# PSUM banks for scores in a fused attention and gated FFN kernel: every score one slot behind an FFN chunk takes the FFN bank, and weight pieces lie three slots apart

## The chip, the cores and the metric

The kernel runs on one core of one Trainium2 chip. The number that counts is the device time of one launch in microseconds (us). The kernel before takes 1467.96 us (median of 3 runs, 1467.65 to 1468.54). All the rows come from one profiled execution of it, whose own time is 1467.12 us; its span from the first to the last instruction is 1465.3 us.

## The reference

All inputs are float32 in the reference, with batch 4, 3136 positions and model width 256:

```python
scores = (1 / S) * z @ z.T                  # z: (4, 3136, 64)
x = u * (max(scores, 0) ** 2 @ v)           # u, v: (4, 3136, 256)
h = max(x @ w_in, 0)                        # w_in: (256, 1024)
c = conv over positions of h, 3 taps, one filter for each of the 1024 channels
out = (h * sigmoid(c)) @ w_out              # w_out: (1024, 256)
```

## The kernel before, in words

**Tiling.** The queries of a batch are cut into 6 blocks of 512 and a rest of 64. For every block the kernel walks over the 25 key tiles of 128 positions. One key tile of one block is a *slot*, so the main loop has 4 x 6 x 25 = 600 slots, numbered k from 0. Slot 77 is the third slot of the fourth block (77 = 3 x 25 + 2). Products are made from a high and a low part in float32r, three matmuls for one (two for the scores, whose operands hold both parts).

**What one slot does.** The loop at the end of the kernel is a software pipeline written out by hand, and each engine keeps its order. In loop slot k, ScalarE (ACT) and VectorE (DVE) first split the squared score of tile k+2 into its high part `ah` (`split_hi`, L513) and its low part `al` (`split_lo`, a subtraction through the helper on L171). Then ReLU (`relu`, L489) and square (`square`, L504) are made of tile k+3. On TensorE (PE) come the output matmuls of an FFN chunk where one is due (`ffn_out`, L780 to L782), the six `av` matmuls of tile k (`attend`, L535), the two score matmuls of tile k+4 (`scores`, L409 and L410), and last the six input matmuls of an FFN chunk where one is due (`ffn_in`, L705 to L708). Many tiles below the diagonal are not computed: their scores come back turned from memory (DMA transposes), and then the slot has no score matmul.

**The FFN.** The FFN of a block runs in eight chunks of 128 channels during the slots of the next block. `FS = [2, 5, 8, 11, 15, 18, 21, 24]` says in which slot of the block a chunk's `ffn_in` stands. Its result stays in one PSUM bank: ReLU in the next slot, the three taps on it in the two slots after (ACT L744, DVE L749 twice), the sigmoid and the gate four slots behind `ffn_in` (ACT L756, DVE `ffn_gate` L763). The gate is the last that reads the bank.

**PSUM.** There are eight banks: two for `av`, two for the FFN output (`o0`, `o1`), two with the tag `s` and two with the tag `ph`. A score normally takes an `s` bank, which comes free when `split_lo` of its tile is done. FFN chunks take the `ph` banks in turn; so do, at a few places, three small users: `ring_score`, `early` and `rem_scores`. A matmul that opens a bank waits on PE for the last reader of the tile that held it before; behind it in PE's order everything waits.

**The weights.** They arrive as 64-bit floats. 16 pieces of 128 x 256 are converted during the first two blocks by `prep_w`, in five stages in successive slots: stage 0 is two integer operations on DVE (L316, L320), stage 1 two on ACT, stage 2 one or two on DVE (L328, L333), stages 3 and 4 are on GpSimd (POOL) and ACT. `WS` gives each piece's first slot. Its intermediate words lie in SBUF (`wr`) or, for the pieces before slot 22 and those in `W_B`, in a PSUM bank (`wp`). The pieces in `W_A` do the second half of stage 2 on ACT and POOL instead of DVE.

Of the kernel before, what the change touches and what calls it, by code (L numbers as in the profile page):

```python
# [8 lines left out]
F32 = mybir.dt.float32  # L9
# [3 lines left out]
U32 = mybir.dt.uint32  # L13
U64 = mybir.dt.uint64
AF = mybir.ActivationFunctionType
ALU = mybir.AluOpType
# [12 lines left out]
LA, LT, LS = 4, 3, 2  # L29
# [2 lines left out]


K_O = 35
Q0 = 3
C0 = [0, 1, 2, 3, 16, 17, 22, 23, 4, 5, 18, 19, 8, 9, 20, 21, 6, 7, 10, 11, 14, 15, 12, 13, 24]

# [12 lines left out]
WARM = 7  # L50
VO = 4
Z1 = -3
WS = [2, 6, 8, 12, 16, 19, 21, 25, 27, 33, 36, 38, 40, 41, 46, 52]
WST = [0, 1, 1, 2, 3]
W_E = ["GGGGGGGGGGGGGGGG", "AAAAAAAAAAAAAAAA"]
W_C = 7
W_A = [9, 14]
W_B = [6, 7]
SQ = [26, 46]
W_P = 22  # L60

# [18 lines left out]
def kernel(  # L80
# [10 lines left out]
    nc = tc.nc  # L91
# [29 lines left out]
    def own(b, q):  # L121
        return CB if b == 0 and q < Q0 else 0

# [180 lines left out]
    def prep_w(stage, what, i, e3=nc.gpsimd, e4=nc.scalar, bank=None, low=None):  # L304
        t, *me = wst[what, i]
        lo, hi = words(t)
        n = hi.shape[-1]
        if stage == 0:
            if not me:
                x = w_area(1, 3).rearrange("p (a d) -> p a d", a=2)  # L310
                me = [x[:, 0], x[:, 1]]
            m, e = me
            if bank is not None:
                m, e = bank[:, 0, :n], bank[:, 1, :n]
            wst[what, i] = [t, *me, m, e]
            nc.vector.tensor_scalar(  # L316
                out=e.bitcast(U32), in0=hi, scalar1=20, scalar2=0x7FF,
                op0=ALU.logical_shift_right, op1=ALU.bitwise_and,
            )
            nc.vector.tensor_single_scalar(out=m.bitcast(U32), in_=hi, scalar=0xFFFFF, op=ALU.bitwise_and)  # L320
            return
        m, e, pm, pe = me
        if stage == 1:
            m, e = pm, pe
            nc.scalar.activation(e.bitcast(I32), e.bitcast(I32), AF.Relu, scale=2.0**23, bias=ebias)
            nc.scalar.activation(m, m.bitcast(U32), AF.Copy, scale=2.0**-20, bias=1.0)
        elif stage == 2:
            nc.vector.scalar_tensor_tensor(  # L328
                out=e.bitcast(U32), in0=hi, scalar=0x80000000, in1=pe.bitcast(U32),
                op0=ALU.bitwise_and, op1=ALU.bitwise_or,  # L330
            )
            if low is None:
                nc.vector.scalar_tensor_tensor(out=m, in0=lo, scalar=2.0**-52, in1=pm, op0=ALU.mult, op1=ALU.add)  # L333
            else:
                nc.scalar.activation(lo.bitcast(F32), lo, AF.Copy, scale=2.0**-52)
                low.tensor_tensor(out=m, in0=lo.bitcast(F32), in1=pm, op=ALU.add)
        elif stage == 3:
            e3.tensor_tensor(out=m, in0=m, in1=e, op=ALU.mult)
        elif what == "in":
            m = m.rearrange("p (a n) -> p a n", a=DC)  # L340
            a, b = (w[:, :, i * P : (i + 1) * P] for w in (wih, wil))
            copy(e4, a, m)
            sub(nc.gpsimd, b, m, a)
        else:
            copy(e4, woh[:, i], m)
            sub(nc.gpsimd, wol[:, i], m, woh[:, i])
# [50 lines left out]
    def scores(k):  # L397
        blk, j, tr = at_slot(k)
        if tr or held(k) or side(k) == CB - 1:
            return  # L400

        if k < K_O and k % 2:
            tag, n = ("ph", 2) if k < NJ else (f"o{k // 2 % 2}", 1)
        else:
            tag, n = "s", 2
        s = ps.tile([P, 512], F32, tag=tag, name="s", bufs=n)
        w, c = slice(j * P, (j + 1) * P), own_cols(k)
        r = zq[blk][:, c] if blk == 1 else turned(zq[blk][:, c])
        nc.tensor.matmul(s[:, c], lhsT=zh[:, w], rhs=r, start=True, stop=False)  # L409
        nc.tensor.matmul(s[:, c], lhsT=zl[:, w], rhs=r, start=False, stop=True)  # L410
        sc[k] = s

    rl, pl, dq, dd, tp = {}, {}, {}, {}, {}


# [11 lines left out]
    def part(k):  # L427
# [3 lines left out]
        if x is not None and x < CB - 1:  # L431
            src = rl[k][:, (x + 1) * P : (x + 2) * P if x else NB]
        elif x is None and not (tr or r < (Q0 if b == q == 0 else q + 1) or (r == QB and q >= RB)):
            src = rl[k]
# [257 lines left out]
    ph, hb, cc, gg, po = {}, {}, {}, {}, {}  # L692
# [125 lines left out]
    ev = defaultdict(lambda: tuple([] for _ in range(6)))  # L818
# [7 lines left out]
    def at(slot, cls, fn, *args):  # L826
        ev[slot][cls].append((fn, args))
# [3 lines left out]
    for q in zs[2:]:  # L831
        s = min(C0.index(j) for j in range(q * CB, min(q * CB + CB, NJ))) - LA - 3
# [11 lines left out]
    for b in range(1, B):  # L844
        k0 = (b * QB - 1) * NJ
        for q in range(QB + 1):
            s = k0 - (QB - 2 - q) * NJ + (12 if q % 2 == 0 else 4)
            if q == QB - 2:
                s = k0 + 6
            elif q == QB - 1:  # L850
                s = k0 + NJ + 6
            elif q == QB:
                s = k0 + 9
            if b == 1 and q < 2:
                s = (Q0 - QB) * NJ + NJ + k0 + 4 + 8 * q
            at(s - 4, POST, load_z, b, q)
            at(s, POST, prep_z, q)
        last = {j: i for i, (j, _) in enumerate(ent[b - 1][QB - 1])}
        for j in range(0, NJ, 2):
            s = k0 + max(last[j] + 2, last.get(j + 1, 0) + 2, V0 + V1 * j // NJ)  # L860
            if j == NJ - 1:
                s = k0 + V0 - 2
# [5 lines left out]
    for blk in range(1, NBLK):  # L868
        s = blk * NJ + E3
# [4 lines left out]
    for blk in range(PK, NBLK):  # L874
        s = blk * NJ + (R_E if blk % QB == RB else E24[blk % QB])
# [5 lines left out]
    n = len(RN) - 1  # L881
    for b in range(B):
# [9 lines left out]
        for i in range(n + 1):  # L892
            s = k5 + (R_J + 2 * i + R_L * (i == n - 1) // 2 if i < n else R_D + 1) + 1
# [23 lines left out]
    for i, (_, what, f) in enumerate(sorted(need)):  # L917
        s = WS[i]
        at(s - 4, POST, load_w, what, f)
# [11 lines left out]
    for blk in range(NBLK - 1):  # L931
        k0 = (blk + 1) * NJ
        at(k0, C_GATE, gate_x, blk, G)
        at(k0 + XS, C_XS, split_x, blk, (V, G))
        for f in range(FC):
            s = k0 + FS[f]
            if s == NS - 1:
                break
            at(s, POST, ffn_halo, blk, f)
            at(s, PE1, ffn_in, blk, f)  # L940
            at(s + RELU, C_RELU, ffn_relu, blk, f)
            at(s + RELU, C_RELU, ffn_keep, blk, f)
            at(s + TAP, C_TAP, ffn_tap, blk, f)
            at(s + ST1, C_ST1, ffn_conv, blk, f, 1)
            at(s + ST2, C_ST2, ffn_conv, blk, f, 2)
            before_end(s + SIG, C_SIG, ffn_sig, blk, f)
            before_end(s + GATE, C_G, ffn_gate, blk, f, G)
            before_end(s + GHI, C_HI, ffn_hi, blk, f, A)
            before_end(s + GHI, PE1, ffn_lo, blk, f, G)
            before_end(s + OUT0, PE0, ffn_out, blk, f, 0)  # L950
            before_end(s + OUT1, PE0, ffn_out, blk, f, 1)
        if blk < NBLK - 2:
            at(s + EVAC, C_EV, evac, blk)
            at(s + EVAC + 2, POST, store, blk)
    at(NS - 2, POST, rem_x)

    def tail():
        blk, pre = NBLK - 1, NBLK - 2
# [97 lines left out]
    with tc.manual_schedule():  # L1056
# [8 lines left out]
        n = FC * KW  # L1065
# [6 lines left out]
        for k in range(-LA, NS):  # L1072
            e = ev[k]
            run(e[PRE])
            early = k + LT < K_O
            if early and 0 <= k + LT:
# [81 lines left out]
```

## Time and profile before

| what | value |
|---|---|
| median of 3 runs | 1467.96 us |
| the profiled execution: its own time / its span | 1467.12 / 1465.3 us |
| PE busy | 1451.6 us (99% of the span), 6781 matmuls |
| ACT, DVE, POOL busy | 1178.5, 1143.4, 864.0 us |
| granted TensorE clock | 1.000 of full speed |
| DMA | mean 140 GB/s |

Busy times overlap. A matmul is shown with its whole way through the array (0.38 us for 512 columns) while the next one already starts; so two starts that lie up to 0.38 us apart show no idle time, and short waits are read from the distance between starts.

### The profile page before, as it was taken

To read this page: it belongs to the slowest core of one execution; us is meant where nothing else is said; L and a number is where in the kernel's file an instruction comes from. 1 tells how busy PE (TensorE), PEld (TensorE's weight loads), DVE (VectorE), ACT (ScalarE), POOL (GpSimd) and SP (SyncE) were. 2 spreads that over 40 slices of the span, in tenths; PEclk is the share of its full clock that TensorE was granted. 3 is DMA by queue.
4 is the path that set the end of the run, shared out by engine and by line. 5 is a ranking of instruction groups with operands and counts; after the bars stand their busy time and mean duration, and the time that the engine had idled before them with its cause. 6 is when DMAs were issued, how large, how long until landed. Compare 5 with 4: busy or idle time off the path is not lost.

```text
span 1465.3 us, 22715 instructions
## 1 busy us (share of the span) xinstructions
PE 1451.6 (99%) x6781; PEld 1260.7 (86%) x6781; DVE 1143.4 (78%) x1776; ACT 1178.5 (80%) x2246; POOL 864.0 (59%) x1218
## 2 busy tenths in 40 slices
PE   9999999999999999999999999999999999999998
PEld 7778888888888888888888888888888888888887
DVE  8998777768787777767777877876778777787677
ACT  8878887878877877878888788787887777878767
POOL 7875656447866654545776654554586654554433
PEclk9999999999999999999999999999999999999999
DMA  6544666865445556678444555586644446567621
GB/s 198 164 132 104 153 142 156 169 150 138 147 134 142 135 132 157 138 149 178 133 149 132 138 140 134 140 172 138 157 149 137 132 122 150 129 132 168 133 63 37
DMA packets 432380, 205.24 MB, mean 140 GB/s; under 512 B 330753, under 2 KB 411905, under 8 KB 432257
## 3 DMA queue, kind: packets, MB, share of 16 engines
q1 hardware_dynamic: 431584, 203.40, 56.9%
q8 instruction: 53, 0.87, 0.3%
q14 instruction: 71, 0.57, 0.1%
q10 hardware_dynamic: 672, 0.40, 0.1%
HBM read 36.59 MB, written 86.90 MB: 84 GB/s over the span
## 4 chain that ended last, share of the span: by engine, by line
PE 87%; POOL 4%; ACT 3%; DVE 3%; issue 2%; DMA 0%; SPq 0%; ACTq 0%; POOLq 0%; DVEq 0%
PE av L535 46%; PE ph L708 5%; PE o L780 5%; PE o L782 5%; PE ph L705 5%; PE o L781 5%; PE ph L706 5%; PE s L409 4%; PE s L410 4%; PE av L617 1%; DVE ph L749 1%; POOL vv L171 1%; POOL pl L439 1%; ACT ph L744 1%; DVE al L171 1%
## 5 line engine op out<-in xcount | busy, mean ns | idle before, releaser
L535 PE MATMUL av<-ah,vv 128*128 128x512 f32 x2400 | 708.7, 379 | 1.4 <-ACT ah L513 0.7
L171 DVE TENSOR_TENSOR al<-s,ah 128x512 fp32r<-128x512 f32 x576 | 397.5, 690 | 225.4 <-PE av L535 116.8
L535 PEld LDWEIGHTS av<-ah,vv 128*128 128x128 f32 x2400 | 449.5, 189 | 64.9 <-ACT ah L513 1.1
L535 PE MATMUL av<-al,vv 128*128 128x512 f32 x1152 | 437.0, 379 | 0.4
L171 POOL TENSOR_TENSOR gl<-hb,gh 128x512 fp32r<-128x512 f32 x192 | 245.3, 1277 | 157.1 <-ACT gh L174 149.3
L749 DVE SCALAR_TENSOR_TENSOR ph<-hb,cw,ph 128x512 f32<-128x512 f32 x384 | 286.8, 747 | 9.4 <-ACT ph L744 9.0
L439 POOL COPY pl<-t 128x1024 uint16<-128x1024 uint16 (+1 forms) x257 | 260.9, 1017 | 2.2 <-DMA dq<-pl 1.1
L535 PEld LDWEIGHTS av<-al,vv 128*128 128x128 f32 x1152 | 217.7, 189 | 32.6 <-DVE al L171 1.8
L504 DVE TENSOR_TENSOR s<-s,t 128x512 f32<-128x512 f32 x275 | 191.8, 697 | 61.5 <-ACT t L489 60.8
L489 ACT ACTIVATE t<-s 128x512 f32<-128x512 f32 x277 | 166.1, 599 | 64.1 <-PE s L410 60.0
L513 ACT CAST ah<-s 128x512 fp32r<-128x512 f32 x277 | 163.3, 590 | 59.8 <-DVE s L504 59.5
L756 ACT ACTIVATE ph<-ph 128x512 f32<-128x512 f32 (+1 forms) x200 | 115.4, 577 | 78.1 <-DVE ph L749 74.7
L739 POOL COPY halo<-hb 128x2 f32<-128x2 f32 x160 | 31.1, 194 | 240.6 <-ACT hb L734 232.2
L484 ACT ACTIVATE s<-tp 128x512 f32<-128x512 f32 x278 | 165.3, 596 | 4.9 <-DMA tp<-dd 3.0
L705 PE MATMUL ph<-xh,wih 128*128 128x512 f32 x384 | 145.8, 380 | 1.1 <-DVE hb L763 1.1
L780 PE MATMUL o<-gh,wol 128*128 128x512 f32 x384 | 145.9, 380 | 0.0
L782 PE MATMUL o<-gl,woh 128*128 128x512 f32 x384 | 145.5, 379 | 0.0
L706 PE MATMUL ph<-xh,wil 128*128 128x512 f32 x384 | 145.5, 379 | 0.0
L781 PE MATMUL o<-gh,woh 128*128 128x512 f32 x384 | 145.5, 379 | 0.0
L744 ACT ACTIVATE ph<-hb,cw 128x512 f32<-128x512 f32 x192 | 133.7, 696 | 6.2 <-POOL halo L739 0.4
L763 DVE TENSOR_TENSOR hb<-ph,hb 128x512 f32<-128x512 f32 x192 | 131.8, 686 | 5.1 <-ACT ph L756 0.7
L734 ACT ACTIVATE hb<-ph 128x512 f32<-128x512 f32 x192 | 114.2, 595 | 17.7 <-PE ph L708 16.3
(138 smaller groups left out, 2091.3 us busy)
## 6 DMA issues: line engine op xcount, KB each, us to landing
dq<-pl SPq DMA_DIRECT2D x232, 256.0 KB, 2.7
st<-in_v_dram SPq DMA_DIRECT2D x48, 256.0 KB, 3.1
ut<-in_u_dram SPq DMA_DIRECT2D x24, 512.0 KB, 4.1
out_dram<-ob SPq DMA_DIRECT2D x19, 512.0 KB, 3.8
st<-in_z_dram SPq DMA_DIRECT2D x24, 256.0 KB, 3.2
sh<-sc SPq DMA_DIRECT2D x44, 128.0 KB, 2.4
dd<-pl SPq DMA_DIRECT2D x69, 64.0 KB, 2.2
dd<-pl SPq DMA_DIRECT2D x23, 192.0 KB, 2.4
```

The lines of the kernel that those rows point to most:

```text
L171: eng.tensor_tensor(out=out, in0=a, in1=b.bitcast(F32), op=ALU.subtract)
L439: nc.gpsimd.tensor_copy(pl[k], src.bitcast(U16).rearrange("p (n h) -> p h n", h=2))
L484: nc.scalar.activation(sc[k][:, :NB], tp[k], AF.Square, scale=SC1**-0.5)
L489: nc.scalar.activation(rl[k], sc[k][:, :NB], AF.Relu, scale=SC1)
L504: nc.vector.tensor_tensor(out=s, in0=s, in1=rl[k], op=ALU.mult)
L535: nc.tensor.matmul(o, lhsT=w[:, j, d], rhs=pairs(r), start=first and i == 0, stop=last and i == len(ops) - 1)
L705: nc.tensor.matmul(o, lhsT=wih[:, dc, w], rhs=pairs(xh[blk][:, dc]), start=(dc == 0), stop=False)
L706: nc.tensor.matmul(o, lhsT=wil[:, dc, w], rhs=pairs(xh[blk][:, dc]), start=False, stop=False)
L749: nc.vector.scalar_tensor_tensor(out=c, in0=hb[blk, f][:, k : e + k], scalar=cw[:, f, k : k + 1], in1=c, op0=ALU.mult, op1=ALU.add,)
L780: nc.tensor.matmul(o, lhsT=wol[:, f, d], rhs=pairs(h), start=(f == 0), stop=False)
L781: nc.tensor.matmul(o, lhsT=woh[:, f, d], rhs=pairs(h), start=False, stop=False)
L782: nc.tensor.matmul(o, lhsT=woh[:, f, d], rhs=pairs(l), start=False, stop=(f == FC - 1))
```

## The change

Scores: in the new function body of `scores`, a tile whose score stands in the slot directly behind an `ffn_in` (that slot is put into the set `gaps`) takes a `ph` bank instead of an `s` bank, in all blocks and for tiles above 35. A slot is taken out of the set again where one of the three small users of `ph` stands in it or beside it. In the built program 63 scores change their bank: most blocks with computed scores have some in their slots 0, 3, 9, 16 and 19. What each of them waits for changes with it: one in a `ph` bank waits for the gate (`ffn_gate`) of the FFN chunk that held that bank; the next `ffn_in` into that bank, two slots on, waits for `split_lo` of the score; and the scores that stay in `s` banks meet a turn that is one slot longer. No matmul, vector or scalar operation is added or removed, and PE's order stays as it was.

Weights: pieces 8, 9, 10, 12, 13 and 14 (counted from 0) start in other slots: 27, 33, 36, 40, 41, 46 become 28, 31, 35, 41, 44, 47. Pieces 8 and 9 keep their intermediate words in a `ph` bank too. For the pieces in `W_A` the mantissa is written to SBUF in stage 1.

```diff
+GAPS = 99
-WS = [2, 6, 8, 12, 16, 19, 21, 25, 27, 33, 36, 38, 40, 41, 46, 52]
+WS = [2, 6, 8, 12, 16, 19, 21, 25, 28, 31, 35, 38, 41, 44, 47, 52]
-W_B = [6, 7]
+W_B = [6, 7, 8, 9]
...
         if stage == 1:
-            nc.scalar.activation(m, m.bitcast(U32), AF.Copy, scale=2.0**-20, bias=1.0)
+            nc.scalar.activation(me[0] if low else m, m.bitcast(U32), AF.Copy, scale=2.0**-20, bias=1.0)
...
-                low.tensor_tensor(out=m, in0=lo.bitcast(F32), in1=pm, op=ALU.add)
+                low.tensor_tensor(out=m, in0=lo.bitcast(F32), in1=m, op=ALU.add)
...
-        if k < K_O and k % 2:
+        if k - LA in gaps and k > K_O:
+            tag, n = "ph", 2
+        elif k < K_O and k % 2:
             tag, n = ("ph", 2) if k < NJ else (f"o{k // 2 % 2}", 1)
         else:
             tag, n = "s", 2
...
+    gaps = set()
...
             at(s, PE1, ffn_in, blk, f)
+            if blk < GAPS:
+                gaps.add(s + 1)
...
+    for s in list(gaps):
+        if any(fn in (ring_score, early, rem_scores) for x in (s - 1, s, s + 1) for c in ev[x] for fn, _ in c):
+            gaps.discard(s)
```

On DVE, from slot 41 to the start of slot 43, the order before holds the second half of piece 12 and the whole of piece 13 (`al` is the split that frees a score's bank; `wr` are words of a weight piece):

```order
L171 TENSOR_TENSOR al<-s,ah 128x512
L504 TENSOR_TENSOR s<-s,t 128x512
L328 SCALAR_TENSOR_TENSOR wr<-wr 128x256
L333 SCALAR_TENSOR_TENSOR wr<-wr 128x256
L316 TENSOR_SCALAR wr<-wr 128x256
L320 TENSOR_SCALAR wr<-wr 128x256
L171 TENSOR_TENSOR al<-s,ah 128x512
L504 TENSOR_TENSOR s<-s,t 128x512
L749 SCALAR_TENSOR_TENSOR ph<-hb,cw,ph 128x512
L328 SCALAR_TENSOR_TENSOR wr<-wr 128x256
L333 SCALAR_TENSOR_TENSOR wr<-wr 128x256
L171 TENSOR_TENSOR al<-s,ah 128x512
```

In the order now, the same stretch holds piece 12 alone (the changed file's lines are up to 4 higher):

```order
L172 TENSOR_TENSOR al<-s,ah 128x512
L508 TENSOR_TENSOR s<-s,t 128x512
L317 TENSOR_SCALAR wr<-wr 128x256
L321 TENSOR_SCALAR wr<-wr 128x256
L172 TENSOR_TENSOR al<-s,ah 128x512
L508 TENSOR_TENSOR s<-s,t 128x512
L753 SCALAR_TENSOR_TENSOR ph<-hb,cw,ph 128x512
L329 SCALAR_TENSOR_TENSOR wr<-wr 128x256
L334 SCALAR_TENSOR_TENSOR wr<-wr 128x256
L172 TENSOR_TENSOR al<-s,ah 128x512
```

What stands directly ahead of the last split is the same in both: a tap and two operations of a weight piece.

On DVE from slot 31 to 34, before, piece 9 begins near the end of the stretch (`hb<-ph,hb` is the gate of an FFN chunk, `ph<-hb,cw,ph` a tap):

```order
L763 TENSOR_TENSOR hb<-ph,hb 128x512
L171 TENSOR_TENSOR al<-s,ah 128x512
L504 TENSOR_TENSOR s<-s,t 128x512
L749 SCALAR_TENSOR_TENSOR ph<-hb,cw,ph 128x512
L171 TENSOR_TENSOR al<-s,ah 128x512
L504 TENSOR_TENSOR s<-s,t 128x512
L749 SCALAR_TENSOR_TENSOR ph<-hb,cw,ph 128x512
L316 TENSOR_SCALAR wr<-wr 128x256
L320 TENSOR_SCALAR wr<-wr 128x256
L171 TENSOR_TENSOR al<-s,ah 128x512
L504 TENSOR_TENSOR s<-s,t 128x512
L763 TENSOR_TENSOR hb<-ph,hb 128x512
```

Now piece 9 stands two slots earlier there, with its words in a PSUM bank (`wp`):

```order
L767 TENSOR_TENSOR hb<-ph,hb 128x512
L317 TENSOR_SCALAR wp<-wr 128x256
L321 TENSOR_SCALAR wp<-wr 128x256
L172 TENSOR_TENSOR al<-s,ah 128x512
L508 TENSOR_TENSOR s<-s,t 128x512
L753 SCALAR_TENSOR_TENSOR ph<-hb,cw,ph 128x512
L329 SCALAR_TENSOR_TENSOR wr<-wr,wp 128x256
L172 TENSOR_TENSOR al<-s,ah 128x512
L508 TENSOR_TENSOR s<-s,t 128x512
L753 SCALAR_TENSOR_TENSOR ph<-hb,cw,ph 128x512
L172 TENSOR_TENSOR al<-s,ah 128x512
L508 TENSOR_TENSOR s<-s,t 128x512
```

The two operations of stage 0 moved ahead of two splits, and that of stage 2 follows them; behind slot 52 DVE's order is unchanged.

## Rows read from the trace of the kernel before

**Rows 1.** The page's busy times of the engines, share of the span, instructions:

```profile
PE 1451.6 (99%) x6781; PEld 1260.7 (86%) x6781; DVE 1143.4 (78%) x1776; ACT 1178.5 (80%) x2246; POOL 864.0 (59%) x1218
```

**Rows 2.** Waits of PE: total us, times, longest us:

```profile
PE s L409 <- DVE al L171: 2.7, 4, 1.6
```

**Rows 3.** Windows: stretch, length, busy us of each engine (instructions), clock, DMA:

```profile
62.00:98.00 36.00, 33.71 (x151) 27.28 (x149) 34.65 (x61) 29.78 (x62) 24.49 (x37) 1.00 0.46 130
98.00:122.00 24.00, 23.54 (x109) 19.86 (x108) 21.22 (x33) 20.00 (x41) 20.23 (x28) 1.00 0.45 132
```

**Rows 4.** Timeline, a short wait in slot 152: start us, us, instruction:

```profile
358.64 0.69 DVE L171 TENSOR_TENSOR al<-s,ah 128x512 fp32r<-128x512 f32 x1
...
359.39 0.48 PE L409 MATMUL s<-zq,zh 128*128 128x512 f32 x1
...
359.71 0.38 PE L410 MATMUL s<-zq,zl 128*128 128x512 f32 x1
```

**Rows 5.** Timeline, a longer wait in slot 190:

```profile
453.36 0.69 DVE L171 TENSOR_TENSOR al<-s,ah 128x512 fp32r<-128x512 f32 x1
...
453.57 0.38 PE L535 MATMUL av<-al,vv 128*128 128x512 f32 x1
...
454.10 0.48 PE L409 MATMUL s<-zq,zh 128*128 128x512 f32 x1
...
454.42 0.38 PE L410 MATMUL s<-zq,zl 128*128 128x512 f32 x1
```

**Rows 6.** Timeline, slots 75 to 77:

```profile
180.41 0.68 DVE L763 TENSOR_TENSOR hb<-ph,hb 128x512 f32<-128x512 f32 x1
...
181.59 0.38 PE L409 MATMUL s<-zq,zh 128*128 128x512 f32 x1
...
184.94 0.69 DVE L171 TENSOR_TENSOR al<-s,ah 128x512 fp32r<-128x512 f32 x1
...
185.26 0.38 PE L705 MATMUL ph<-xh,wih 128*128 128x512 f32 x1
```

**Rows 7.** Timeline, slot 377:

```profile
898.47 0.69 DVE L171 TENSOR_TENSOR al<-s,ah 128x512 fp32r<-128x512 f32 x1
898.58 0.38 PE L705 MATMUL ph<-xh,wih 128*128 128x512 f32 x1
```

**Rows 8.** Timeline, slot 218:

```profile
520.29 0.69 DVE L171 TENSOR_TENSOR al<-s,ah 128x512 fp32r<-128x512 f32 x1
...
520.92 0.38 PE L705 MATMUL ph<-xh,wih 128*128 128x512 f32 x1
```

**Rows 9.** Timeline, slot 150:

```profile
354.60 0.68 DVE L763 TENSOR_TENSOR hb<-ph,hb 128x512 f32<-128x512 f32 x1
...
355.29 0.38 PE L409 MATMUL s<-zq,zh 128*128 128x512 f32 x1
```

**Rows 10.** Line 316: duration ns min/median/max, first and last start us, forms:

```profile
L316 DVE TENSOR_SCALAR wp<-wr x8: 418/469/506, 15.0 to 57.0; 128x256 uint32<-128x256 uint32 x8
L316 DVE TENSOR_SCALAR wr<-wr x8: 307/476/1310, 61.7 to 126.1; 128x256 uint32<-128x256 uint32 x8
```

**Rows 11.** Timeline, the largest wait, slots 38 and 39:

```profile
88.15 1.31 DVE L316 TENSOR_SCALAR wr<-wr 128x256 uint32<-128x256 uint32 x1
...
90.85 0.51 PE L409 MATMUL s<-zq,zh 128*128 128x512 f32 x1 [1.65 <-DVE al L171]
```

**Rows 12.** Timeline, slots 42 and 43:

```profile
99.89 0.87 POOL L236 CAST zq<-zh 64x512 fp32r<-64x512 f32 x1
...
100.06 1.06 DVE L328 SCALAR_TENSOR_TENSOR wr<-wr 128x256 uint32<-128x256 uint32 x1
...
101.06 1.08 DVE L333 SCALAR_TENSOR_TENSOR wr<-wr 128x256 f32<-128x256 uint32 x1
...
101.49 0.38 PE L705 MATMUL ph<-xh,wih 128*128 128x512 f32 x1
...
102.06 0.67 DVE L171 TENSOR_TENSOR al<-s,ah 128x512 fp32r<-128x512 f32 x1
```

## The prediction

> **What bounds the kernel now.** I read the page's busy times first. PE is busy 99% of the span, the other engines 59 to 80% [rows 1]. So nothing makes this kernel faster but taking away moments in which PE stands, and every new wait of PE is paid in full. Next the list of PE's waits: the one that counts is a score waiting for `split_lo` on DVE, that is for an `s` bank, 2.7 us in four long waits [rows 2]. That list is not the whole bill, since starts are 0.216 us apart where nothing waits (23.54 busy us for 109 matmuls [rows 3]) while one matmul is shown for 0.38 us; a start that comes 0.1 us late shows no idle time. I therefore went on to the timeline and took the distances from start to start.
>
> Two short pieces of it give the price of a late bank. In slot 152 the split ends at 358.64 + 0.69 = 359.33 and the score starts at 359.39: 0.06 us from release to start. It did not come late, yet the next matmul follows 0.32 us behind instead of 0.22, so 0.10 us is lost [rows 4]. In slot 190 the split ends at 454.05; the score starts 0.53 us after the `av` matmul ahead of it, 0.31 late, and again 0.10 is lost behind it [rows 5]. So a bank that comes free x us after the moment at which PE would have opened it costs x + 0.06 + 0.10 us; with x between -0.16 and -0.06 it costs the part of the 0.10 that is not hidden; below that nothing.
>
> Where PE loses time today: between 62 and 98 us, block 1 with weight pieces 8 to 13, 151 matmuls x 0.216 = 32.6 of 36 us; between 98 and 122, 109 x 0.216 = 23.5 of 24 [rows 3]. Some of these matmuls are half as wide, and start to start, slot by slot, the two stretches lose 4.0 and 1.0 us. All later blocks together lose only some 2.5 us at such places, outside the tail. DVE is busy for 34.65 of the first 36 us [rows 3]: there it is the bound.
>
> **The change part by part: scores and chunks in steady state.** No work is added or removed; 63 scores get another releaser, and so do the `ffn_in` two slots behind them. I took from the built program which tile held each bank before, and set the end of its last reader, as the trace has it, against the start on PE. Behind slot 53 all engines keep their order, so the same trace serves for both.
>
> The moved scores themselves mostly have room. In slot 75 the gate ends at 181.09 and the score starts at 181.59, 0.50 us of room [rows 6]. The `s` scores gain a turn: their room grows from 0.1 to 2 us now to 2.5 to 4. What is late next is `ffn_in`, whose bank was free for 4 us before and now waits for the split of the score that stood there two slots earlier. Slot 2 of a block is where DVE and ACT also prepare the next FFN input. In slot 77 the split ends at 185.63 and `ffn_in` starts at 185.26 [rows 6]: 0.37 + 0.16 = 0.53 us. Slots 227 and 527 have the same figures; in 377 it is 899.16 against 898.58, 0.58 + 0.16 = 0.74 [rows 7]. Sum of the four: 2.3 us. In slot 218 the split ends at 520.98 against 520.92: 0.06 + 0.16 = 0.22, and slots 368 and 518 repeat it: 0.7 [rows 8]. In slot 150 a moved score starts at 355.29 and its gate ends at 355.28: 0.15 us, five times (150, 300, 325, 450, 475): 0.75 [rows 9]. Slots 177, 327 and 477 stand as slot 152 does today, 0.10 each, and four more scores (153, 175, 303, 453) lose about 0.04: 0.45 together. Sum: 4.2 us. Against it go today's short waits that the longer turn removes: 152, 302, 452 (0.10 each), 55 (0.26), 205 and 355 (0.15 together): 0.7. The wait in slot 190 and its like in 340 stay: the tile before them in the bank is still two scores back. Net +3.5 us. What would hide a part: a shift of the DVE chain against PE by 0.4 us; I know of none, since DVE's order there is the same and its splits themselves follow PE's `av` matmuls. Bounds: +2.5 (the fifteen small ones cost nothing) to +4.5.
>
> **Block 1.** By the split of slot 40 the pieces 8 to 11 are done, before and now, so a DVE that is busy 96% of the time has the same work to do by then, and the 4.0 us lost there can shrink only by its idle 1.35 us [rows 3] and by operations that take less time. The latter is real but uncertain: an operation on `wr` takes between 0.31 and 1.31 us, median 0.48, one with its result in a PSUM bank always 0.42 to 0.51 [rows 10]. The largest wait, 1.65 us of idle in slot 39, follows one of 1.31 us [rows 11], 0.8 over the median. Pieces 8 and 9 in `ph` banks are safe from that, 10 and 11 meet other neighbours: I take -1.1 (0 to -2.4). Piece 9 stands two slots earlier, 0.8 us ahead of two splits for which slots 32 and 33 still wait in `s` banks; this is paid early and given back by slot 40. The moved scores of slots 34 and 37 want a gate that stands late in its slot on DVE, and the score's own split then starts later: +0.6. Sum to slot 40: -0.5, from -3.0 to +1.5.
>
> Slot 43 is new. Its `ffn_in` starts at 101.49 today; now it waits for the split that ends at 102.06 + 0.67 = 102.73, 1.24 + 0.16 = 1.4 us [rows 12]. That split is late because two operations of a weight piece ahead of it take 1.06 and 1.08 us beside casts of POOL [rows 12]; by the order lists two of the same kind still stand there, of piece 12 now instead of 13. With the median of some 0.48 each the wait would be 0.2. I take 1.2, nearer the row. The Trainium skill (SBUF — State Buffer, section Who interferes with whom) says that a DVE instruction with two SBUF inputs and a GpSimd instruction that reads SBUF share a port pair, and that the one that issues second is fully blocked. The trace agrees with the 1.06 and 1.08 us beside POOL's casts [rows 12]. By that rule the full 1.4 us come back, since POOL's casts are still issued there, and the sum would be 0.2 us higher; without it, 1 us lower.
>
> In slots 44 to 49 the 1.0 us lost today came with pieces 12 and 13 close together; with 13 three slots later most of it goes, and I keep 0.4: -0.6. Slots 50, 52 and 53 get 0.2. The changed stage 1 of the `W_A` pieces writes the same 256 columns to SBUF instead of PSUM: nothing, within 0.1 us on ACT, which is 80% busy; hidden by PE unless DVE waits for it. The moved loads of weight pieces on SP's queue lie four slots ahead of their use as before. Sum for block 1: -0.5 + 1.2 - 0.6 + 0.2 = +0.3, from -4 to +3.5.
>
> **The sum.** +3.5 + 0.3 = +3.8 us on the profiled execution's 1467.12 gives 1470.9. That execution lies 0.84 us below the median of the runs shown (1467.96), and the runs after will be compared with those: 1471.8 us.
>
> **The rivals.** *Block 1 pays for it.* The spread of the pieces takes all 5.0 us of stalls away and slot 43 meets no late split, while the steady cost stands: -5.0 + 3.5 = -1.5, 1466.5 us, no change. For it: block 1 holds two thirds of what PE loses today. Against: DVE's 34.65 of 36 us. *The third bank does its work.* It is the other side: the split of slot 77 and its like end 0.5 us earlier against PE, because ACT writes the turned tiles into `s` banks that now come free sooner, and block 1 runs clear: -5.0 - 0.7 = -5.7, 1462.3 us. It is decided at one point, whether the split of slot 77 still ends after 185.2. Against it: ahead of that split ACT runs without a pause, so a bank that is free sooner does not start it sooner. The Trainium skill (Perfetto Trace Analysis, section Optimization Strategy) says that consistent bubbles on the engine that should be saturated can mean too little PSUM for the next tile. That speaks for this rival; here such bubbles in steady state are 2.5 us, and by the rule 0.7 to 2.5 of them would go. *Block 1 gets worse.* In slots 34 to 46 score and chunk wait for each other's DVE work in the same `ph` banks, each wait delays the ReLU and square that follow, and DVE stands idle where it was saturated: +3.0 over the forecast, 1474.8 us. For it: piece 9 is earlier in the most loaded stretch. That the banks are not used as said is no rival: the built program shows the 63 places.
>
> **How the numbers follow.** The forecast (the sum, 1470.3 to 1473.6) gets 0.60, no net change 0.19, the third bank 0.08, the worse block 1 0.13. 0.2% is 2.9 us, about what a measurement of this kernel can tell from no change: slower means above 1470.9, faster below 1465.0. A fifth of the forecast's chance lies under 1470.9. So slower 0.48 + 0.13 = 0.61, same 0.12 + 0.19 = 0.31, faster 0.08. The range takes in the case of no net change and most of the worse block: 1466.0 to 1474.6, with 0.08 left below and 0.1 above.
>
> **What the profile after would show.** Right: waits of `ph` L709 (`ffn_in`) for DVE `al` in slots 77, 227, 377 and 527 of 0.4 to 0.6 us, and one near 1.2 us in slot 43; the waits of `s` scores in slots 35, 36, 39, 46, 55 and 152 gone; from 122 us to the tail the stretch longer by 3 to 4 us at the same matmul count. Wrong: no wait at slot 77, or block 1 shorter or longer by over 2 us.

## The result, and the profile after

The changed kernel takes 1476.19 us (median of 5 runs, 1475.18 to 1476.48), the kernel before 1467.65 us on the same chip (5 runs, 1467.40 to 1468.54). The ratio is 1.0053, with a 95% interval of 1.0041 to 1.0066: slower by 8.5 us. Forecast were 1471.8 us and a range that ended at 1474.6; the direction came out, the size lies outside. The profiled execution took 1476.48 us, its span is 1474.7 us.

The page's busy times answer to [rows 1]:

```profile
PE 1455.7 (99%) x6781; PEld 1259.3 (85%) x6781; DVE 1145.7 (78%) x1776; ACT 1179.4 (80%) x2246; POOL 864.2 (59%) x1218
```

The instructions are the same in number on every engine. DVE's work grew by 2.3 us. The list of PE's waits answers to [rows 2] (total us, times, longest us):

```profile
PE ph L709 <- DVE al L172: 3.8, 7, 1.2
PE s L412 <- DVE al L172: 3.5, 6, 1.5
...
PE s L412 <- DVE hb L767: 0.4, 1, 0.4
```

`ffn_in` (L709) now waits for splits, seven times; before, the list had no such line. But the scores (L412) wait longer for splits as well, 3.5 instead of 2.7 us. The windows answer to [rows 3]:

```profile
62.00:98.00 36.00, 31.62 (x139) 25.57 (x140) 31.98 (x54) 27.79 (x58) 22.32 (x35) 1.00 0.37 107
98.00:122.00 24.00, 22.11 (x99) 17.85 (x98) 21.87 (x34) 18.13 (x38) 16.79 (x23) 1.00 0.44 132
```

In the same 36 us PE issues 139 matmuls instead of 151, and DVE, which was busy for 34.65, is busy for 31.98: it has more idle time, not less.

From here on, "lost" is the distance from one matmul's start to the next beyond 0.216 us for 512 columns, summed by slot; a long wait comes out some 0.3 us above the idle time that the profile prints. In the two profiled executions slots 26 to 53 (block 1) lose 6.2 us before and 10.6 after, the later slots up to the tail 5.4 and 10.3. The spans differ by 9.4 us where the medians differ by 8.5; some single slots (446, 274, 574) lose anything between 0 and 0.8 us from one profiled execution to the next, also where the kernels do not differ, and the profile of before happened to have nothing at 446.

**The steady places.** Three timelines of after answer to [rows 6, 8, 9] (slots 77, 218, 150):

```profile
189.34 0.69 DVE L172 TENSOR_TENSOR al<-s,ah 128x512 fp32r<-128x512 f32 x1
...
190.09 0.48 PE L709 MATMUL ph<-xh,wih 128*128 128x512 f32 x1 [0.27 <-DVE al L172]
...
190.41 0.38 PE L710 MATMUL ph<-xh,wil 128*128 128x512 f32 x1
```

```profile
525.48 0.69 DVE L172 TENSOR_TENSOR al<-s,ah 128x512 fp32r<-128x512 f32 x1
...
526.23 0.48 PE L709 MATMUL ph<-xh,wih 128*128 128x512 f32 x1
...
526.55 0.38 PE L710 MATMUL ph<-xh,wil 128*128 128x512 f32 x1
```

```profile
359.52 0.68 DVE L767 TENSOR_TENSOR hb<-ph,hb 128x512 f32<-128x512 f32 x1
...
360.26 0.48 PE L412 MATMUL s<-zq,zh 128*128 128x512 f32 x1
```

Each starts 0.06 us behind the end of its releaser (190.03, 526.17, 360.20), and the next matmul stands 0.32 us behind instead of 0.22 (in slot 150 at 360.58): the price rule of the prediction. Lost are 0.53, 0.23 and 0.15 us.

**Block 1.** PE's waits there, from the timeline:

```profile
73.63 0.50 PE L412 MATMUL s<-zq,zh 128*128 128x512 f32 x1 [1.47 <-DVE al L172]
...
79.68 0.50 PE L412 MATMUL s<-zq,zh 128*128 128x512 f32 x1 [0.38 <-DVE hb L767]
...
84.88 0.48 PE L709 MATMUL ph<-xh,wih 128*128 128x512 f32 x1 [1.17 <-DVE al L172]
...
95.92 0.50 PE L412 MATMUL s<-zq,zh 128*128 128x512 f32 x1 [0.96 <-DVE al L172]
...
105.11 0.48 PE L709 MATMUL ph<-xh,wih 128*128 128x512 f32 x1 [1.06 <-DVE al L172]
...
121.59 0.48 PE L412 MATMUL s<-zq,zh 128*128 128x512 f32 x1 [0.41 <-DVE al L172]
```

These are slots 32, 34, 36, 40, 43 and 49; shorter ones of 0.33 and 0.32 us stand in slots 33 and 46. The wait of 1.65 us in slot 39 [rows 11] is gone; these took its place. What DVE does ahead of two of them, and where it stands idle in between:

```profile
64.85 0.70 DVE L508 TENSOR_TENSOR s<-s,t 128x512 f32<-128x512 f32 x1 [0.80 <-ACT t L493]
...
68.12 0.69 DVE L172 TENSOR_TENSOR al<-s,ah 128x512 fp32r<-128x512 f32 x1 [0.64 <-ACT ah L517]
...
71.38 0.68 DVE L767 TENSOR_TENSOR hb<-ph,hb 128x512 f32<-128x512 f32 x1
72.10 0.43 DVE L317 TENSOR_SCALAR wp<-wr 128x256 uint32<-128x256 uint32 x1
72.56 0.43 DVE L321 TENSOR_SCALAR wp<-wr 128x256 uint32<-128x256 uint32 x1
72.89 0.68 DVE L172 TENSOR_TENSOR al<-s,ah 128x512 fp32r<-128x512 f32 x1
...
81.14 0.70 DVE L508 TENSOR_TENSOR s<-s,t 128x512 f32<-128x512 f32 x1 [0.76 <-ACT t L493]
81.75 0.75 DVE L753 SCALAR_TENSOR_TENSOR ph<-hb,cw,ph 128x512 f32<-128x512 f32 x1
82.40 0.77 DVE L317 TENSOR_SCALAR wr<-wr 128x256 uint32<-128x256 uint32 x1
83.09 1.14 DVE L321 TENSOR_SCALAR wr<-wr 128x256 uint32<-128x256 uint32 x1
84.15 0.68 DVE L172 TENSOR_TENSOR al<-s,ah 128x512 fp32r<-128x512 f32 x1
```

The split at 72.89 follows a gate and the first two operations of piece 9, which now stand in this slot; it ends at 73.57 and PE starts at 73.63. The split at 84.15 has 1.9 us of piece 10 directly ahead of it.

The idle times of DVE have two causes. That at 64.85 comes before any new wait of PE: piece 8 starts a slot later now, DVE and ACT have less to do there, get ahead, and ACT waits for a score that PE makes in its turn. Before, DVE stood 0 us there, and 0.49 at the place of 68.12. The run piece8_only, which moves piece 8 alone, has both idle times. First ACT's row in the changed kernel, then DVE's in piece8_only:

```profile
64.22 0.60 ACT L493 ACTIVATE t<-s 128x512 f32<-128x512 f32 x1 [0.70 <-PE s L413]
```

```profile
65.11 0.70 DVE L508 TENSOR_TENSOR s<-s,t 128x512 f32<-128x512 f32 x1 [0.70 <-ACT t L493]
...
68.33 0.69 DVE L172 TENSOR_TENSOR al<-s,ah 128x512 fp32r<-128x512 f32 x1 [0.59 <-ACT ah L517]
```

The idle time at 81.14 comes behind PE's wait in slot 34: there the score itself is late, then ACT's `t`, then DVE.

### The profile page after: what moved, and what is told of

It reads as the page before. It is cut to its first block, busy times and chain, and to the rows that moved or that the text cites. A ratio compares the mean times of both kernels' runs of the same rounds, so it can differ in the third digit from the quotient of the medians.

```text
span 1474.7 us, 22671 instructions
## 1 busy us (share of the span) xinstructions
PE 1455.7 (99%) x6781; PEld 1259.3 (85%) x6781; DVE 1145.7 (78%) x1776; ACT 1179.4 (80%) x2246; POOL 864.2 (59%) x1218
## 4 chain that ended last, share of the span: by engine, by line
PE 84%; ACT 6%; DVE 4%; issue 2%; POOL 2%; DMA 1%; SPq 0%; ACTq 0%; POOLq 0%; DVEq 0%
PE av L539 44%; PE ph L709 5%; PE ph L712 5%; PE o L786 5%; PE o L784 5%; PE o L785 5%; PE ph L710 5%; PE s L412 4%; PE s L413 4%; PE av L621 2%; DVE al L172 1%; DVE ph L753 1%; ACT t L493 1%; ACT xh L175 1%; ACT ah L517 1%
## 5 line engine op out<-in xcount | busy, mean ns | idle before, releaser
L709 PE MATMUL ph<-xh,wih 128*128 128x512 f32 x384 | 147.4, 384 | 5.0 <-DVE al L172 3.8
L738 ACT ACTIVATE hb<-ph 128x512 f32<-128x512 f32 x192 | 114.3, 596 | 17.1 <-PE ph L712 15.8
```

Source lines behind the costliest of these rows:

```text
L709: nc.tensor.matmul(o, lhsT=wih[:, dc, w], rhs=pairs(xh[blk][:, dc]), start=(dc == 0), stop=False)
```

## The experiments

All are the changed kernel with other constants, and some with one line changed as shown; "old" and "new" are the two lists `WS` of the diff above, and `W_B` is that of before unless it is said. The changed stage 1 of the `W_A` pieces is in all of them. Each was compared with the kernel before on the same chip. The lost times are those of one profiled execution of each kernel.

**Which half, and which blocks.** Four kernels:

```diff
weights_only:      WS new, W_B = [6, 7, 8, 9], GAPS = 0
banks_only:        WS old, GAPS = 99
block1_only:       WS new, W_B = [6, 7, 8, 9], GAPS = 1   # moved scores in block 1 alone
banks_later_only:  WS old
-            if blk < GAPS:
+            if 1 <= blk < GAPS:
```

> The new weight slots and the new W_B, every score in its old bank (GAPS = 0). Theory A, the weight slots cost in block 1 by themselves: piece 9 two slots earlier meets the stretch in which DVE is already the bound, and pieces 8 and 9 keep a ph bank from ffn_in. Then slots 30 to 33 lose 2 us more than before, as in the changed kernel, nothing changes behind slot 55, and the time is +2 to +4 us on before. Theory B, the banks cost in block 1: slots 30 to 33 recover in the slots behind them, and the time is within 1 us of before. Theory C, only both together cost: slots 30 to 33 lose 2 us and slots 36 to 49 win as much: within 1 us too, but with the loss of slots 30 to 33 in the trace.

> The moved scores in all blocks, the weight pieces in their old slots and banks. The steady cost that was read off the trace before (+3.5 us net behind slot 53) comes back to within 0.5 us, slot 77 losing 0.53. Theory A: block 1 stays where it was or better, so +3 to +4 us in all. Theory B: block 1 loses 3 to 4 us as in the changed kernel, +7 to +8 in all. Theory C: in between, and slot 43 loses over 1 us.

> The new weight slots, scores moved only behind the FFN chunks of block 0, that is in block 1 (GAPS = 1). The steady cost goes, block 1 stays as in the changed kernel: all theories +4 to +5 us on before, 3.5 to 4.5 less than the changed kernel. If the time falls by more than 5, the later blocks cost more than the banks' waits say; by less than 3, less.

> Old weight slots, scores moved only behind the FFN chunks of blocks 1 and later. The steady cost by itself: +3.5 us on before (+2.5 to +4.5), block 1 as before to within 0.2 us. A rival says that the small extra waits of the changed kernel in slots 274, 446 and 574 (0.9 us together) belong to the banks too: then +4.4, with waits in those three slots; if they are chance of the execution, they are elsewhere or gone.

Measured, against 1467.21 us: weights_only 1472.88 (ratio 1.0040, 1.0027 to 1.0052), banks_only 1471.99 (1.0032, 1.0019 to 1.0044), block1_only 1471.57 (1.0029, 1.0017 to 1.0040), banks_later_only 1471.52 (1.0028, 1.0017 to 1.0040). What PE lost, in us:

| slots | before | after | weights_only | banks_only | block1_only | banks_later_only |
|---|---|---|---|---|---|---|
| 30 to 40 | 4.2 | 6.3 | 8.0 | 3.6 | 6.4 | 4.0 |
| 41 to 50 | 1.1 | 3.2 | 2.8 | 1.6 | 3.2 | 1.1 |
| 26 to 53 | 6.2 | 10.6 | 11.7 | 6.2 | 10.6 | 6.4 |
| 54 to 598 | 5.4 | 10.3 | 6.0 | 11.1 | 6.1 | 10.0 |

So everything in block 1 costs 4.4 us (block1_only), the banks of the later blocks cost 4.3 (banks_later_only), and the two add up to the 8.5 within 0.2. In block 1 the banks by themselves cost nothing: slot 34 loses 0.7, 37 0.9, 40 0.7 and 43 1.3 us more, and 35, 36, 39, 46 and 49 give 0.4, 0.5, 1.9, 0.7 and 0.2 back. The new weight slots cost 5.5 us there without the banks and 4.4 with them; but 1.7 of the 5.5 are matmuls at half the clock, which the changed kernel does not have (shown below with piece 10), so without that they cost 3.8.

Slot by slot, the changed kernel against banks_only shows what the new weight slots cost beside the moved scores: 2.1 us in slots 30 to 33, 0.7 in 34 to 40 and 1.6 in 46 to 50. The changed stage 1 of the `W_A` pieces is in banks_only too, where block 1 loses no more than before.

**Which piece.** One move each, all scores in `s` banks (GAPS = 0), the other starts old:

```diff
piece8_only:   -27, 33, 36, 38   +28, 33, 36, 38
piece9_only:   -27, 33, 36, 38   +27, 31, 36, 38
piece10_only:  -27, 33, 36, 38   +27, 33, 35, 38
late_pieces:   -40, 41, 46       +41, 44, 47
wb_only:       WS old, -W_B = [6, 7]  +W_B = [6, 7, 8, 9]
```

> The kernel before with one number changed: piece 8 starts in slot 28 instead of 27. Theory A1, a DVE that works ahead of need loses time by waiting for ACT: with piece 8 a slot later DVE reaches the square of slot 28 before ACT's t, idles 0.8 us there and 0.6 two splits later, and this time is missing at slots 32 to 40: slot 32 loses 0.5 to 1.4 us more and block 1 in all +0.7 to +1.5. Theory A2, piece 9 does the harm: block 1 within 0.3 us of before.

> The kernel before with one number changed: piece 9 starts in slot 31 instead of 33. Theory A1: slots 32 and 33 lose 0.5 us more in all, slots 35 to 39 win it back, block 1 within 0.5 us. Theory A2, two pieces too close to the chunk's splits: slots 32 and 33 lose 1 to 1.7 us more, and slots 35 to 40 do not win it back, since DVE then waits for ACT and PE: block 1 +1 to +2.

> The kernel before with piece 10 in slot 35 instead of 36. Its two operations of stage 0 then stand ahead of the split of slot 36 for which that slot's score waits. With the weight slots alone this place lost 3.7 us, before 0.7. If piece 10 does that by itself, slot 36 loses 2 to 3 us and slot 39 wins 1.2 back: block 1 +0.7 to +2. If it needs pieces 8 and 9 earlier as well, slot 36 loses under 1.5 and block 1 stays within 0.5 us.

> The kernel before with pieces 12, 13 and 14 in slots 41, 44 and 47 (before 40, 41, 46), all else as before. The forecast's step for slots 44 to 49: the 1.0 us lost there falls to 0.4 and slots 30 to 40 stay as they are: -0.6. The opposite, which the run with the weight slots alone suggests: each piece that stands in the slot ahead of a split for which a score waits costs 0.3 to 1.5 us there, slots 45 to 49 lose 2 to 2.7 us instead of 1.0: +1 to +1.7.

> The kernel before with pieces 8 and 9 keeping their words in a ph bank (W_B), old slots, old banks for scores. If the ph bank itself costs (a chunk's ffn_in that waits for the piece's stage 2, and operations on PSUM that are never faster than 0.42 us), slots 30 to 36 lose 0.5 us or more beyond before. If the bank helps because POOL cannot hold these operations up, block 1 loses up to 0.5 us less. The forecast had -0.25.

Measured: piece8_only 1469.22, ratio 1.0006 (0.9997 to 1.0015); piece9_only 1468.18, 0.9998 (0.9989 to 1.0007); late_pieces 1469.66, 1.0010 (1.0001 to 1.0019); all three against 1468.37. piece10_only 1468.50, 1.0009 (1.0000 to 1.0018), and wb_only 1470.38, 1.0016 (1.0007 to 1.0026), against 1467.55. The times of single moves lie at the edge of what can be told apart; the lost time in slots 26 to 53 of the profiled executions is sharper: piece 8 +0.6, piece 9 -0.5, piece 10 +2.0, pieces 12 to 14 +1.6, the `ph` bank for the words of 8 and 9 at their old slots +4.6 us. But the profiled executions of piece10_only (1470.06 us) and wb_only (1472.15) are 1.6 and 1.8 us longer than the median of their kernel: both hold a stretch at half the clock, shown next, and five of the ten executions of piece10_only took 1467.6 to 1468.1 us. Piece 9, the move I thought of as the risk, gains here: it takes 1.0 us from the wait in slot 39.

Piece 10 alone shows how a move of one slot can cost 2 us. Timeline of DVE and PE in the profiled execution (start us, us, instruction, idle before it):

```profile
81.07 0.64 DVE L317 TENSOR_SCALAR wr<-wr 128x256 uint32<-128x256 uint32 x1
81.63 1.35 DVE L321 TENSOR_SCALAR wr<-wr 128x256 uint32<-128x256 uint32 x1
82.89 0.68 DVE L172 TENSOR_TENSOR al<-s,ah 128x512 fp32r<-128x512 f32 x1
...
83.63 0.39 PE L412 MATMUL s<-zq,zh 128*128 128x256 f32 x1 [2.04 <-DVE al L172]
...
89.17 0.69 DVE L172 TENSOR_TENSOR al<-s,ah 128x512 fp32r<-128x512 f32 x1 [2.46 <-PE av L539]
```

Before, nothing of a weight piece stood ahead of this split; it ended at 81.22 and the score started at 81.28. Now stage 0 of piece 10 stands there, 1.8 us, and PE, which keeps its order, stands for 2.04 us. After that DVE stands for 2.46 us, since its next split comes behind PE's `av` matmuls. The windows show a second loss behind the wait (the number behind the five engines is the granted clock); the last row is weights_only:

```profile
84.00:86.00 2.00, 2.00 (x9) 1.66 (x8) 2.00 (x5) 1.69 (x4) 0.99 (x2) 0.73 0.03 8
86.00:88.00 2.00, 2.00 (x6) 1.61 (x5) 0.70 (x2) 1.98 (x4) 1.37 (x3) 0.50 0.69 221
88.00:90.00 2.00, 2.00 (x9) 1.67 (x9) 0.69 (x1) 0.43 (x1) 0.10 (x1) 0.92 0.46 159
```

```profile
86.00:88.00 2.00, 2.00 (x6) 1.64 (x5) 1.55 (x4) 1.97 (x5) 0.92 (x3) 0.50 0.04 12
```

PE stood from 81.6 to 83.6 and then worked without a pause; in the window from 86 to 88 us the granted clock is 0.50, that is 1.2 instead of 2.4 GHz, and from 84.8 to 88.2 most starts lie 0.43 us apart instead of 0.216. From start to start this is 1.7 of the 4.1 us lost in slots 36 and 37. Slot 39 gives 1.2 back, so without the lower clock the move costs 0.3 of the 2.0 us. The changed kernel doesn't have this part: its clock is 1.00 in the windows shown above. There the score of slot 36 no longer waits for that split; the chunk's `ffn_in` behind it does, for 1.17 us.

For the words of pieces 8 and 9 in a `ph` bank, wb_only:

```profile
74.98 0.42 DVE L317 TENSOR_SCALAR wp<-wr 128x256 uint32<-128x256 uint32 x1
...
76.96 0.68 DVE L767 TENSOR_TENSOR hb<-ph,hb 128x512 f32<-128x512 f32 x1
...
77.79 0.77 PE L709 MATMUL ph<-xh,wih 128*128 128x512 f32 x1 [3.20 <-DVE hb L767]
```

The words of piece 9 (74.98) take the `ph` bank whose turn it is, so the `ffn_in` of slot 33 gets the other one, and that is held until the gate of the chunk just ahead of it, which ends at 77.64. PE stands for 3.20 us; behind it the granted clock is 0.50 to 0.54 from 78 to 84 us, some 3 of the 4.6 us. At the new slots the words' bank costs less: the `ffn_in` of slot 30 waits for the piece's last operation on them (L334), and 0.34 us are lost.

The single moves add up to 3.8 us, the weight slots as changed cost 5.5. Where the rest is:

```diff
early_three:        28, 31, 35 new, 40, 41, 46 old, GAPS = 0
moves_only:         WS new, GAPS = 0
weights_free_bank:  WS new, GAPS = 99
```

> Pieces 8, 9 and 10 in the new slots 28, 31 and 35 together; pieces 12 to 14, the banks of the pieces' words and the banks of the scores as before. One at a time these moves changed what PE loses from start to start in slots 26 to 53 by +0.63, -0.47 and +2.04 us. Theory A, the prices add: +2.2 us there, about 1470 us, slot 36 at 3.3 and slot 39 at 0.8 us. Theory B, the missing part of the five and a half us of the weight slots is an interplay of these three: +3 to +4 us, slot 32 at 1.5 or more (the prices of pieces 8 and 9 there add on top of each other) and slot 39 not below 0.8.

> All six pieces in the new slots, but pieces 8 and 9 keep their words in SBUF (W_B as before), and all scores in s banks. Theory A, the words in a PSUM bank are what is missing between the sum of the moves (+3.8 us) and the weight slots as changed (+5.5 us): +3.8 us in slots 26 to 53, no loss in slots 30 and 33, about 1471.3 us. Theory B, the bank does nothing for the loss and the moves make it among themselves: +5 to +6 us, about 1473 us. Theory C, the bank helps, as I forecast (its operations take 0.42 to 0.51 us): over +6 us.

> All six pieces in the new slots, the words of pieces 8 and 9 in SBUF as before, all scores in s banks as before (the run weights_free_bank kept the new banks of the scores, against what was written of it). Theory B of that run, the moves make the loss among themselves: +3.2 us of the three early ones together and +1.6 of the three late ones, +4.8 us in slots 26 to 53, about 1472 us. Theory A, the words in the ph bank are the missing part: +3.8 us, about 1471.0 us, and slot 36 below 3 us.

early_three took 1470.38 us against 1467.16 (1.0020, 1.0011 to 1.0030), moves_only 1472.39 against 1467.36 (1.0031, 1.0019 to 1.0044). The kernel weights_free_bank kept the scores' new banks, against what its expectation says; so it tells only what the words' bank costs in the changed kernel: 1474.92 (1.0054, 1.0039 to 1.0069), within the intervals of the changed kernel. In slots 26 to 53 early_three loses 3.2 us more than before, where the three single moves gave 2.2; moves_only 5.0 more; the words' bank adds 0.5 without and 0.6 with the scores' banks. So 3.2 + 1.6 + 0.5 = 5.3 of the 5.5 are named.

In the 3.2, the 5.0 and the 5.5, as in piece 10's 2.0, 1.7 us is the lower clock behind the wait of slot 36; the profiled executions of weights_free_bank and of the changed kernel do not have it there. Not every execution of a kernel does: three of the ten of early_three took 1468.8 us at a granted clock of 1.000, the other seven 1470.1 to 1471.2 at 0.998; one of the six of moves_only took 1470.4 at 1.000, the others 1472.2 to 1472.6 at 0.999. Without it 1.5 + 1.6 + 0.5 = 3.6 of 3.8 are named. So the prices of the single moves cannot simply be added up to the 4.4 us that the same slots cost in the changed kernel, where the moved scores have changed the waits; piece 9 is the only single move that was also tried there (no_gap41_p9 below). The 1.0 us of interplay sits mostly in slot 39: piece 9 and piece 10 each take about 1 us from its 1.95 (0.97 and 0.78 are left), and together they take it only once (0.79 is left).

**Slot 43.** Are POOL's casts (L237) what makes its split late? The casts go four slots earlier; and the moved score behind it is taken back, alone and with piece 9 early:

```diff
casts_moved:   WS old, GAPS = 1
-  POST, query, blk)
+  - 4 * (blk == 2), POST, query, blk)
no_gap41:      WS old, GAPS = 1
+    gaps.discard(41)
no_gap41_p9:   as no_gap41, -27, 33, 36  +27, 31, 36
```

> Old weight slots, scores moved behind the chunks of block 0 alone, and POOL's two casts of the next block's queries four slots earlier, in slot 38 instead of 42. If the two slow operations of slot 42 (1.06 and 1.08 us) are slow because of these casts, they take about 0.5 each now, and slot 43 loses 0.1 to 0.4 us instead of 1.3; block 1 then loses 5 instead of 6.2 us, and the time is 1 us below before. If something else holds them, slot 43 loses 1.3 as it does with the casts in place, and the time is that of before.

> Old weight slots, scores moved only behind the chunks of block 0, and the score of slot 41 left in its s bank, so that the ffn_in of slot 43 waits for no split. Slot 43 loses nothing (1.3 with the score moved), slots 34 to 40 stay as with all moved scores (3.6 us), slots 45 to 49 lose between 0 and 1.0: block 1 loses 4.9 to 5.9 us instead of 6.2, and the time is 0.3 to 1.3 us below before. If the wait only goes elsewhere, 6.2 and no change.

> The same with piece 9 in slot 31, which alone took 0.5 us from block 1. If the two add up, block 1 loses 4.2 to 5.2 us, and the time is 1 to 2 us below before: the best version so far. If piece 9 ahead of the gate that slot 34's moved score waits for only fills the same DVE time, it is that of the run without it.

casts_moved took 1469.48 us against 1468.37 (1.0007, 0.9998 to 1.0016). Slot 43 lost 1.8 us, more than with the casts beside it (1.3 in banks_only, the nearest run to compare it with):

```profile
100.58 0.49 DVE L329 SCALAR_TENSOR_TENSOR wr<-wr 128x256 uint32<-128x256 uint32 x1
100.61 1.33 POOL L443 COPY pl<-t 128x1024 uint16<-128x1024 uint16 x1
101.00 1.22 DVE L334 SCALAR_TENSOR_TENSOR wr<-wr 128x256 f32<-128x256 uint32 x1
...
102.14 0.68 DVE L172 TENSOR_TENSOR al<-s,ah 128x512 fp32r<-128x512 f32 x1
...
102.87 0.48 PE L709 MATMUL ph<-xh,wih 128*128 128x512 f32 x1 [1.49 <-DVE al L172]
```

L329 is short now, but L334 takes 1.22 us beside a copy of POOL that moved into the place of the casts. The casts were not the only neighbour, and taking them away freed nothing. So what makes the two operations slow stays open. The Trainium skill (SBUF — State Buffer, section Who interferes with whom) says that a DVE instruction with two SBUF inputs contends with a GpSimd instruction that reads SBUF. The row of L334 (two inputs in SBUF, 1.22 us beside a copy that reads SBUF) agrees, but it doesn't separate POOL from what else may be late there.

no_gap41 took 1467.17 against 1467.55 (0.9997, 0.9989 to 1.0006): slot 43 loses nothing, block 1 0.4 us less than before. no_gap41_p9 took 1467.78 (1.0004, 0.9995 to 1.0012): piece 9's gain does not come on top. Slot 39 is already free of its wait; slots 32 and 33 lose 1.5 us more than in no_gap41, slot 37 gives 0.9 back, and block 1 loses 0.6 us more in all. No version tried is measurably faster than the kernel before.

## Why the prediction was wrong, step by step

**The steady banks: right.** Forecast +3.5 us; banks_later_only measured +4.3 (its interval reaches from 2.5 to 5.9), and the named places make +3.8. Slots 77, 227 and 527 lose 0.53 each, 377 loses 0.77 (forecast 0.74), 218 and its like 0.23, 150 and its like 0.15, 177 and its like 0.10, as the prediction had them; 152 and its like, 55, 205 and 355 are free. Mis-sized were 153, 303 and 453, where I put 0.04 and found 0.14: the bank came late enough for the whole 0.10 behind the start. The other 0.5 us stand at slots that also vary from one execution to the next and stay open. The rival of the third bank fell here: the split of slot 77 still ends behind the moment at which PE would have opened the bank.

**Slot 43: right.** Forecast +1.2, measured 1.3. Two operations of piece 12 stand ahead of the split, as it said, and take 0.94 and 1.24 us (those of piece 13 took 1.06 and 1.08 before). That POOL's casts hold them is not shown: casts_moved has a slow one without the casts, and in the changed kernel the second one runs beside a copy.

**Block 1 up to slot 40: the step that failed.** It said that DVE has the same work to do by the split of slot 40, so the lost time "can shrink only by its idle 1.35 us" and by shorter operations, and that piece 9's place "is paid early and given back by slot 40": -0.5. Measured is +2.2 (30 to 40: 4.2 to 6.3 us). The work is the same: from the split that ends at 61.82 us to the one that slot 40's score waits for (61.97 to 95.87 us after), DVE runs 50 operations and is busy for 30.3 us before and 30.0 after. But its idle time in between, which the step took for something that could only shrink, rose from 1.3 to 4.0 us, as it did in the windows (1.35 to 4.02).

It rose in two ways. Piece 8 a slot later leaves DVE without work at 64 us, and everything behind, up to the split of slot 32, ends later by as much; piece8_only has this by itself (slot 32 loses 1.1 instead of 0.4 us). And a split that comes late stops PE, PE's late scores make ACT's `t` late, and DVE then stands for these.

"Given back by slot 40" holds only where a later wait shrinks by as much. For piece 9 alone it did, as forecast: slots 32 and 33 lose 0.8 us more, and slots 35, 36 and 39 return 0.4, 0.3 and 1.0 (piece9_only). In the changed kernel the moved scores had already taken the wait of slot 39 away (from 2.0 to 0.04 us lost in banks_only). Beside moved scores piece 9 loses 0.6 us in block 1 (no_gap41_p9 against no_gap41) instead of gaining 0.5, and the wait of slot 32 (1.47 us in the changed kernel) was paid and stayed paid. The forecast did not see that both halves of the change draw on the same wait. Pieces 8 and 10, which it treated as neutral, cost something by themselves as well (0.6 us, and 0.3 without the lower clock); what each costs beside the moved scores no run shows.

The second half of that step, -1.1 us for operations that take less time, came in part and bought nothing. Up to slot 40 the 15 operations of pieces 8 to 11 take 8.6 us instead of 9.4, but DVE stands idle for longer than it saves. (The 0.42 to 0.51 us of [rows 10] hold for the first operation with its words in a PSUM bank; the second took 0.47 to 0.54.) Behind slot 40 the operations get longer. The groups of DVE's operations on SBUF words in after (instructions | busy us, mean ns | idle before):

```profile
L321 DVE TENSOR_SCALAR wr<-wr 128x256 uint32<-128x256 uint32 x6 | 4.4, 735 | 0.0
...
L334 DVE SCALAR_TENSOR_TENSOR wr<-wr 128x256 f32<-128x256 uint32 x5 | 4.1, 821 | 0.0
L317 DVE TENSOR_SCALAR wr<-wr 128x256 uint32<-128x256 uint32 x6 | 3.8, 635 | 0.0
L329 DVE SCALAR_TENSOR_TENSOR wr<-wr 128x256 uint32<-128x256 uint32 x6 | 3.5, 587 | 0.0
```

That is 15.8 us for 23 operations, 0.69 each; the same 23, those of pieces 10 to 15, took 13.8 us before. All DVE operations of the 16 pieces take 34.4 us now and took 32.9.

**Slots 44 to 49: the same failure.** Forecast -0.6, since piece 13 stands three slots later. Measured is +0.8: these slots lose 1.8 instead of 1.0 us. late_pieces has this move alone, and slots 41 to 50 lose 2.8 instead of 1.1 us: 1.5 in slot 46 and 0.9 in 49. Spread out, each piece stands ahead of another split:

```profile
108.96 1.45 DVE L334 SCALAR_TENSOR_TENSOR wr<-wr 128x256 f32<-128x256 uint32 x1
...
111.16 0.45 PE L412 MATMUL s<-zq,zh 128*128 128x512 f32 x1 [1.23 <-DVE al L172]
...
119.41 0.48 PE L412 MATMUL s<-zq,zh 128*128 128x512 f32 x1 [0.67 <-DVE al L172]
```

**The bound.** I gave block 1 +3.5 as the upper end and "the worse block 1" 0.13. It came out at +4.4 (2.2 up to slot 40, 1.3 in slot 43, 0.8 and 0.2 behind it), by a mechanism close to that rival's (DVE idle where it was saturated), but not by its cause: scores and chunks in the same banks cost nothing there by themselves (banks_only), the pieces moved beside them did.

## What to carry to other kernels

In a loop in which engine A waits for B, B for C and C for A, a busy share of 96% does not make B a throughput bound whose delays even out: here B's idle time tripled with the same operations. Price each moved operation at the next instruction that another engine waits for behind it, not by the sum of work up to a later point. Two changes that each take away the same wait take it away only once. Work packed into a slot in which nobody waits can be better than the same work spread evenly (late_pieces lost 1.6 us more). A bank given to a second user changes two waits, that of the new user and that of the old one two turns later; the slack of both can be read from the trace before, here to 0.1 us at every place that was named, where the order of the engines stays the same.

## What the runs showed of the hardware that was not expected

- PE that stood for 2.04 us (piece10_only) or 3.20 us (wb_only) in the middle of a saturated stretch was granted 0.50 of its clock for several us afterwards, 1.7 us of extra loss in the first case. It did not come in every execution of such a kernel (early_three: seven of ten). No lower clock shows behind the 1.47 us of the changed kernel or the 1.65 us of the kernel before.
- The two DVE operations of a piece's first stage (128 x 256 words) took between 0.27 and 1.40 us in these kernels where they wrote their words to SBUF, and 0.42 to 0.61 us where they wrote them to a PSUM bank.
